# One K load cut into six: seven eighths of the row in one load, the last eighth in a load of 112 rows and four loads of 4 rows

## The chip, the cores and the metric

One core of a Trainium2 chip runs the kernel. The metric is the device time in microseconds (us) of one execution, as the median of several runs. Lower is better.

## The reference

For two batch entries with one token each, a gate mixes an attention block over a long cache (32 heads, 16384 cached positions, head size 128) with a small two-layer MLP.

```python
def _A_ref(x, k_cache, v_cache, wq, wo):
    q = (x @ wq).reshape(B, Sq, H, Dh).transpose(0, 2, 1, 3)
    scores = jnp.einsum("bhqd,bhkd->bhqk", q, k_cache) * (Dh ** -0.5)
    p = _softmax(scores, axis=-1)
    o = jnp.einsum("bhqk,bhkd->bhqd", p, v_cache)
    return o.transpose(0, 2, 1, 3).reshape(B, Sq, H * Dh) @ wo

def _B_ref(x, w1, w2, w3, w4):
    h = _gelu(_layernorm(x) @ w1)
...
    x1 = x + hs
    return x1 + _gelu(_layernorm(x1) @ w3) @ w4

g = _sigmoid((x * gate_w).sum(-1, keepdims=True))
return g * _A_ref(...) + (1 - g) * _B_ref(...)
```

All inputs are bf16. The K cache and the V cache hold 2 x 32 x 16384 x 128 numbers each, 268 MB each, and every one of them is read once.

## The kernel before

The attention is cut into 32 **units**. A unit is one batch entry `s` (0 or 1) of one pair of heads `i` (0 to 15), and its K and its V are 8 MB each. One load brings such a block to the 128 partitions: 64 KB lie in a row of DRAM for each partition, so the load has 128 rows of 64 KB. Units 0 and 1 (pair 0) are written out by hand, together with the MLP; the loop of L895 runs over the other 15 pairs, two units each; a hand-written tail holds the last V.

For a unit, VectorE transposes K in eight chunks (`dve_scores`, L640): a chunk is one eighth of each row (32 of its 256 positions, 8 KB). TensorE multiplies each transposed chunk with the query (`pe_scores`, L663), eight matmuls a chunk. There are two buffers `kt`, so that transpose number n waits for the scores of chunk n - 2. Unit 1 takes its chunks in the order of the row, so the last eighth is its last chunk. The scores are then transposed back (L647), reduced to a maximum, and turned into weights (`exponent`, L685); the product with V is L713, the projection with `wo` L758.

**The order of the loads.** All large loads are issued by SyncE (SP), on one DMA queue, and each waits on SP until its destination is free. Up to the loop they are: `wq`, `w1`, `w2`, K of unit 0 (L249), `w3`, K of unit 1 (L839), `w4` (issued in `ln.dma`, called at L844). K of unit 1 waits for the fourth transpose of unit 0 (`tr3`, L837) and for the last readers of `w1` and `w2`, whose place it takes; `w4` waits for the matmuls with `w3` (`linear`, L843; its matmuls are L531). In the loop each unit's turn is: K (L906), after the fourth transpose of the unit just before it (`tr3`; the first K of the loop thus waits for unit 1's fourth transpose), then the V of the pair before (L908), after the matmuls with the V that was there, then, once a pair, `wo` (L911, 32 rows of 16 KB to every fourth partition). ACT issues three tiny loads at the start, for the two rows of x and for the gate's row (`xrow`, issued in L82): each has 4 rows of 512 bytes, to partitions that lie 32 apart.

**What waits for K of unit 1.** The first transpose of unit 1 (L640, called at L860) waits for the semaphore `kl1` to reach 16. Behind it on VectorE stand the other transposes of unit 1, the reciprocal of `invert(u0)` (L708) and an addition (L865). The load that SP issues next but one, K of pair 1, batch 0 (L906), waits for unit 1's fourth transpose. The matmuls with `w4` (L870) stand on TensorE behind the scores of unit 1's first seven chunks.

**The tail.** The last V comes in four pieces of 128, 64, 48 and 16 positions of the row (L938), then `wo` for the last two heads in three loads (L946 to L948). The first two pieces go through L713, and VectorE's L781 and L787 reduce what they gave; the last two pieces go through L996. Then come the last projection (L758), the copies to the output row and its store.

Of the kernel before, what the change touches and what calls it, by code (L numbers as in the profile page):

```python
# [88 lines left out]
def kernel(  # L89
# [16 lines left out]
    P = nc.NUM_PARTITIONS  # L106
    B, Sq, D = A_x.shape
    _, H, Sk, Dh = A_k_cache.shape
# [8 lines left out]
    NJ = 2 * Sk // P  # L117
    CT = 32
    NCK = NJ // CT
    GT = 16  # L120
    NG = NJ // GT
    Q4 = 4
# [19 lines left out]
    def S(name):  # L142
        if name not in sems:
            sems[name] = (tc if name in ("fin", "st") else nc).alloc_semaphore(name)
        return sems[name]
# [59 lines left out]
    def region(cell, elements):  # L205
        return mem[:, cell * CELL : cell * CELL + elements]
# [4 lines left out]
    k_rows = A_k_cache.rearrange("b (g t) s d -> b g (t s d)", t=2)  # L211
# [3 lines left out]
    def unit_rows(rows, hp, s):  # L215
        if isinstance(hp, int):
            flat = rows[s, hp : hp + 1, :]
        else:
            flat = rows[s, bass.ds(hp, 1), :]
        return flat.rearrange("o (p x) -> (o p) x", p=P)  # L220
# [7 lines left out]
    def wait(engine, name, value):  # L228
        if isinstance(value, int) and value == 0:
            return  # L230
        engine.wait_ge(S(name), value)
# [7 lines left out]
    with tc.tile_critical(sync_engine=mybir.EngineType.Activation, no_gpsimd_drain=True):  # L239
        PE, DVE, ACT, POOL, SP = nc.tensor, nc.vector, nc.scalar, nc.gpsimd, nc.sync  # L240
# [10 lines left out]
        for b, row in enumerate((A_x[0, 0], A_x[1, 0], gate_w)):  # L251
# [9 lines left out]
                out=ident_f[:], in_=ident_f[:], compare_op=ALU.not_equal, fill=1.0, base=0,  # L261
# [10 lines left out]
        for k in range(2):  # L272
# [14 lines left out]
                out=lmat[:].rearrange("p (g h k) -> p g h k", h=2, k=4),  # L287
                in_=hm2[:].unsqueeze(1).unsqueeze(3).to_broadcast([P, P // 8, 2, 4]),
# [3 lines left out]
        for h in range(2):  # L292
# [4 lines left out]
                    out=place[:, at : at + P].rearrange("p (g k) -> p g k", k=2 * QP)[:, :, 0 : HB + 1 : HB],  # L297
                    in_=ident_f[:, h * HALF : (h + 1) * HALF].rearrange("p (g k) -> p g k", k=QP)[:, :, 0:B],
# [6 lines left out]
                out=ident_s[:], in0=ident_f[:], scalar1=-scale, scalar2=None, op0=ALU.mult  # L305
# [6 lines left out]
                out=rep1[:], in_=ident_f[:].rearrange("p (c k) -> p k c", k=QP), axis=AX.X, op=ALU.add  # L312
# [6 lines left out]
                out=mask4[:], in_=ident_f[:].rearrange("p (c k) -> p c k", k=QP), axis=AX.X, op=ALU.add  # L319
# [3 lines left out]
        for g in range(Q4):  # L323
# [3 lines left out]
                    out=rep4[:, g, :].rearrange("p (a k) -> p a k", k=QP),  # L327
# [13 lines left out]
                out=hsel[:], in_=rep1[:, 0:8].rearrange("p (h k) -> p h k", k=4), axis=AX.X, op=ALU.add  # L341
# [179 lines left out]
        def linear(actT, w, R, N, act_key, w_key, banks, out_keys):  # L521
# [7 lines left out]
            def one(n):  # L529
# [19 lines left out]
                out=tsc[:],  # L549
                in_=oacc2[:].rearrange("p a (m k e) -> p (a m) e k", k=QP, e=2),  # L550
# [6 lines left out]
                out=qTb[:], in_=tsc[:].rearrange("p (c k) -> p c k", k=QP)[:, :, 0:B]  # L557
# [15 lines left out]
        for e in range(2):  # L573
            rows = slice(e * HALF, (e + 1) * HALF)
# [3 lines left out]
                    out=qd[rows],  # L578
                    in_=R_ps[rows].rearrange("p (hp e v b) -> p e hp b v", e=2, v=4, b=B)[:, e],
# [24 lines left out]
        def chunk_ids(s):  # L604
            low, high = list(range(NCK // 2)), list(range(NCK // 2, NCK))
            return high + low if K_CELL[s] == 0 else low + high

        def k_view(s):
            return region(K_CELL[s], NJ * Dh).rearrange("p (j d) -> p j d", d=Dh)
# [9 lines left out]
        def pool_unit(n):  # L619
            wait(POOL, f"sc{NCK - 1}", 0 if n.first else n.after(-1))  # L620
            i, s = n.i, n.s
            dst = qw[s][:, :, NG - 1 : NG - 1 + QP * (Q4 - 1) + 1 : QP]
            row = qd[:, i, s, :] if isinstance(i, int) else qd[:, bass.ds(i, 1), s, :].rearrange("p o v -> p (o v)")
            POOL.tensor_tensor(  # L624
                out=dst,
                in0=row.unsqueeze(2).to_broadcast([P, 4, Q4]),
                in1=mask4[:].unsqueeze(1).to_broadcast([P, 4, Q4]),
                op=ALU.mult,
            ).then_inc(S("qwd"), 1)

        def dve_scores(u, first=0, last=NCK):
            s = u.s
            for n, c in list(enumerate(chunk_ids(s)))[first:last]:
                if n == 0:
                    wait(DVE, f"kl{s}", u.landed)
                if n >= 2:
                    wait(DVE, f"sc{n - 2}", u.after(1))
                else:
                    wait(DVE, f"sc{n + 6}", u.after(0))
                DVE.transpose(  # L640
                    out=kt[n % 2][:],
                    in_=k_view(s)[:, c * CT : (c + 1) * CT, :].rearrange("p j d -> p (j d)").bitcast(FP32),
                ).then_inc(S(f"tr{n}"), 1)
            if last < NCK:
                return
            wait(DVE, f"sc{NCK - 1}", u.after(1))
            DVE.transpose(out=st[:].rearrange("p j r -> p (j r)"), in_=sps[s][:]).then_inc(S("stT"), 1)  # L647
            wait(DVE, "stT", u.after(1))
            DVE.tensor_reduce(out=m_t[:], in_=st[:, :, 0:NG], axis=AX.XY, op=ALU.max).then_inc(S("mx"), 1)  # L649

        def pe_scores(u, first=0, last=NCK):
            s = u.s
            if first == 0:
                wait(PE, "qwd", u.after(1))
                wait(PE, "stT", 0 if u.first else u.after(-1))
            for n, c in list(enumerate(chunk_ids(s)))[first:last]:
                wait(PE, f"tr{n}", u.after(1))
                ktb = kt[n % 2][:].bitcast(BF16).rearrange("p (j w k e) -> p j w k e", j=CT, w=2, k=QP, e=2)
                for half in range(CT // GT):
                    m = c * (CT // GT) + half  # L660
                    for v in range(4):
                        w, e = divmod(v, 2)
                        ins = PE.matmul(  # L663
                            sps[s][:].rearrange("p (j k) -> p j k", k=QP),
                            lhsT=qw[s][:, v, NG - 1 - m : NG - 1 - m + P],
                            rhs=ktb[:, half * GT : (half + 1) * GT, w, :, e],
                            start=(n == 0 and half == 0 and v == 0),
                            stop=(n == NCK - 1 and half == CT // GT - 1 and v == 3),
                        )
                ins.then_inc(S(f"sc{n}"), 1)  # L670
# [158 lines left out]
        for key in ("qd", "mask4", "qw0", "qw1"):  # L829
# [6 lines left out]
        pe_scores(u0, 0, NCK // 2 - 1)  # L836
        wait(SP, "tr3", 1)  # L837
        ln.wait("SP", ln.needs([], ["w1", "w2"]))
        SP.dma_start(out=region(1, NJ * Dh), in_=unit_rows(k_rows, 0, 1)).then_inc(S("kl1"), 16)  # L839
        layernorm_T(x1T[:], xn2T[:], "ln2", "x1T", "xn2T")  # L840
        dve_scores(u0, NCK // 2)
        pe_scores(u0, NCK // 2 - 1, NCK - 1)
# [7 lines left out]
                out=tsc[:, 0:FQ],  # L850
                in_=oacc2[:, :, 0:half].rearrange("p a (i c) -> p c a i", c=FC),
# [5 lines left out]
        exponent(u0)  # L857
        ln.op("POOL", lambda: POOL.memset(tsc[:], 0.0), writes=["tsc"])
        pool_unit(u1)
        dve_scores(u1, 0, NCK // 2)  # L860
        pe_scores(u1, 0, NCK // 2 - 1)
        total(u0)
# [23 lines left out]
                out=brow[:], in0=brow[:], scalar1=omgrow[:, 0:1], scalar2=None, op0=ALU.mult  # L886
# [50 lines left out]
        for n, size in enumerate(PIECES):  # L937
            SP.dma_start(  # L938
                out=region(V_CELL, NJ * Dh)[:, at * Dh : (at + size) * Dh],
                in_=unit_rows(v_rows, HP - 1, 1)[:, at * Dh : (at + size) * Dh],  # L940
# [24 lines left out]
                out=rinv2[:], in0=rinv2[:], scalar1=g_rep[:, 1:2], scalar2=None, op0=ALU.mult  # L965
# [39 lines left out]
        for h in range(2):  # L1005
# [12 lines left out]
            out=out.rearrange("b s (h g c) -> g (b s) h c", h=2, g=Q4), in_=out_row[0 : P - HB + 1 : HB, :]  # L1018
# [37 lines left out]
```

## Time and profile before

| | |
|---|---|
| three runs, median (lowest to highest) | 1331.53 us (1331.51 to 1331.89) |
| the profiled execution's own time | 1331.57 us |
| its span, from its first to its last instruction | 1329.7 us |
| read from DRAM | 572.53 MB, 431 GB/s over the span |
| VectorE busy | 710.1 us (53%) |
| TensorE busy, and its mean granted clock | 824.7 us (62%), 0.801 |
| three stretches from the table by windows: 0 to 20, 130 to 1290, 1290 to 1326 us | DMA share 1.00, 1.00, 0.95 |

The DMA share is the mean busy share of the core's 16 DMA engines. A load of 128 rows puts 8 rows on each engine.

The trace also holds each packet of the DMA queues: its queue, its start, its duration and its size. The views only sum them up, but the list can be read directly. In it a load's row is one packet, and each engine closes its share of a load with a packet of 4 bytes, so that a load of 128 rows leaves 16 of these. On an engine a packet starts about 4 ns before the recorded end of the one before it, so the packets of one engine can be strung together. The list's clock runs 10.52 us ahead of that of the views (the last 4-byte packet of unit 1's K at 99.99 us there, the transpose that waits for it at 89.47 us here). What it shows, in ns:

| load | its 16 closing packets, from the earliest |
|---|---|
| `w2` (third load) | 0 18 25 44 75 88 100 102 114 134 135 195 264 279 299 354 |
| K of unit 0 | 0 17 25 43 75 97 100 102 114 150 263 279 299 354 1145 1656 |
| K of unit 1 | 0 32 33 35 73 91 102 120 183 273 289 310 344 1173 1596 1687 |
| last V, second piece | 0 83 166 263 265 321 336 417 1156 1624 1634 1650 1683 1697 1850 1934 |

| packet | median duration, ns | number |
|---|---|---|
| 65536 bytes | 2422 | 8192 |
| 57344 bytes (rows of `w3` and `w4`) | 2118 | 256 |
| 16384 bytes (among them all of `wo` in the loop) | 611, highest 624 | 864 |
| 12288 bytes | 461 | 128 |
| 4096 bytes | 159 | 128 |
| 4 bytes, closing | 9 | 1440 |
| instructions' queue, 16384 bytes | 1009 to 1221 | 8 |

From the earliest closing packet of `w3` to that of unit 1's K are 19348 ns, and to those of `w3` and `w4` from the load before each 16909 and 16938 ns; from that of the second piece of the last V to that of the third (12288 bytes a row) 3687 ns.

The 12 packets of the three tiny loads lie on four of the engines, the same four for all three loads; in the row of `w2` these four are the engines at 0, 25, 195 and 299.

### The profile page before, as it was taken

How to read it: one execution, taken by the hardware profiler on the slowest of the kernel's cores; microseconds unless marked ns; L12 is line 12 of the kernel's file. 1: busy time of each engine (PE TensorE's matmuls, PEld its weight loads, DVE VectorE, ACT ScalarE, POOL GpSimd, SP SyncE). 2: the span in 40 equal slices, each digit the busy share in tenths (PEclk: the TensorE clock that was granted, in tenths of full speed). 3: DMA queues.
4: the chain of work that ended last, by engine and by line, in shares of the span. 5: the costliest groups of instructions: out<-in, count | busy, mean ns of one | idle time of the engine just before them, and what ended most of it. 6: DMA issues, size and time to landing. Idle time of an engine off the chain costs nothing.

```text
span 1329.7 us, 14080 instructions
## 1 busy us (share of the span) xinstructions
PE 824.7 (62%) x6060; PEld 379.8 (29%) x6060; DVE 710.1 (53%) x712; ACT 105.2 (8%) x165; POOL 15.9 (1%) x47
## 2 busy tenths in 40 slices
PE   2356576665666656567665657656566766656765
PEld 0123232232332223233232323223232322323323
DVE  2365466554556654456565445665444665545561
ACT  0010000000000000000000000000000000000000
POOL 0100000000000000000000000000000000000000
PEclk9587888777888777788877778877778887778885
DMA  9999999999999999999999999999999999999998
GB/s 410 439 422 434 445 424 438 430 430 438 430 438 430 438 430 440 428 440 428 440 426 442 424 444 424 444 424 438 430 430 438 430 438 430 440 428 440 428 440 346
DMA packets 11573, 572.68 MB, mean 431 GB/s; under 512 B 1472, under 2 KB 1740, under 8 KB 1996
## 3 DMA queue, kind: packets, MB, share of 16 engines
q1 hardware_dynamic: 11520, 572.53, 99.6%
q8 instruction: 8, 0.13, 0.0%
q10 hardware_dynamic: 44, 0.01, 0.0%
q14 instruction: 1, 0.01, 0.0%
HBM read 572.53 MB, written 0.00 MB: 431 GB/s over the span
## 4 chain that ended last, share of the span: by engine, by line
DMA 68%; DVE 16%; PE 11%; issue 3%; another core or an unknown queue 1%; POOL 0%; SPq 0%; ACT 0%; POOLq 0%; ACTq 0%
DMA mem<-in_A_k_cache_dram 66%; DVE kt L640 16%; PE S L663 10%; DMA mem<-in_A_v_cache_dram 2%; PE oacc L713 0%; PE ot L531 0%; SPq L906 0%; PE R L996 0%; POOL qw L267 0%; POOL pt L269 0%; DVE st L647 0%; DVE part L787 0%; POOL ln_rstd L471 0%; PE arow L758 0%
## 5 line engine op out<-in xcount | busy, mean ns | idle before, releaser
L663 PE MATMUL S<-kt,qw 128*128 128x512 bf16 x2048 | 544.6, 415 | 265.3 <-DVE kt L640 265.0
L640 DVE STREAM_TRANSPOSE kt<-mem 128x2048 f32<-128x2048 f32 x256 | 570.3, 2282 | 168.8 <-DMA mem<-in_A_k_cache_dram 118.6
L663 PEld LDWEIGHTS S<-kt,qw 128*128 128x128 bf16 x2048 | 194.7, 104 | 601.6 <-issue 292.4
L713 PE MATMUL oacc<-mem,pt 128*8 128x512 bf16 x2032 | 120.2, 390 | 4.3 <-DMA mem<-in_A_v_cache_dram 4.3
L685 ACT ACTIVATE pt<-st,nb 64x256 bf16<-64x256 f32 x64 | 90.1, 1408 | 283.9 <-DVE nb L699 283.4
L731 PE MATMUL ot<-hsel,red 128*128 128x2 f32 x480 | 76.1, 289 | 54.7 <-DVE red L787 54.7
L731 PEld LDWEIGHTS ot<-hsel,red 128*128 128x128 f32 x480 | 73.6, 238 | 69.8 <-DVE red L787 69.8
L781 DVE TENSOR_SCALAR part<-oacc,maskr 128x128 f32<-128x128 f32 x31 | 10.9, 351 | 140.7 <-PE oacc L713 140.7
L674 ACT ACTIVATE Dm<-ident_s,m 128x128 f32<-128x128 f32 x32 | 12.8, 401 | 875.5 <-DVE m L649 875.5
L704 PE MATMUL R<-rs,lmat 128*128 128x1 f32 x64 | 18.4, 357 | 79.1 <-ACT pt L685 79.1
L713 PEld LDWEIGHTS oacc<-mem,pt 128*8 128x8 bf16 x2032 | 47.2, 88 | 64.5 <-issue 5.4
L708 DVE RECIPROCAL rinv<-R 128x1 f32<-128x1 f32 x32 | 5.4, 168 | 109.5 <-PE R L704 109.5
L647 DVE STREAM_TRANSPOSE st<-S 128x512 f32<-128x512 f32 x32 | 22.9, 717 | 70.0 <-PE S L663 70.0
L676 PE MATMUL R<-Dm,ones_f 128*128 128x128 f32 x64 | 15.6, 326 | 54.4 <-ACT Dm L674 54.4
L814 DVE TENSOR_SCALAR oa<-ot,hm 128x8 f32<-128x8 f32 x30 | 6.8, 226 | 78.9 <-PE ot L731 78.9
L704 PEld LDWEIGHTS R<-rs,lmat 128*128 128x128 f32 x64 | 15.8, 306 | 84.9 <-ACT pt L685 84.7
L758 PE MATMUL arow<-wo,OT 128*17 128x128 bf16 x960 | 28.3, 310 | 10.5 <-DVE OT L819 10.5
L685 ACT ACTIVATION_READ_ACCUMULATOR pt<-st,nb 64x1 f32 x64 | 30.7, 479 | 0.0
L676 PEld LDWEIGHTS R<-Dm,ones_f 128*128 128x128 f32 x64 | 9.5, 188 | 70.2 <-ACT Dm L674 70.2
L758 PEld LDWEIGHTS arow<-wo,OT 128*17 128x17 bf16 x960 | 24.6, 132 | 11.3 <-issue 11.3
L787 DVE SCALAR_TENSOR_TENSOR part<-oacc,maskr,part 128x128 f32<-128x128 f32 x62 | 21.8, 351 | 2.2
L624 POOL TENSOR_TENSOR qw<-qd,mask 128x16 bf16<-128x16 f32 (+1 forms) x32 | 8.3, 264 | 1117.7 <-PE S L663 1117.7
(114 smaller groups left out, 128.6 us busy)
## 6 DMA issues: line engine op xcount, KB each, us to landing
mem<-in_B_w_dram SPq DMA_DIRECT2D x2, 7168.0 KB, 34.6
wo<-in_A_wo_dram SPq DMA_DIRECT2D x15, 512.0 KB, 25.2
mem<-in_B_w_dram SPq DMA_DIRECT2D x2, 2048.0 KB, 28.4
mem<-in_A_v_cache_dram SPq DMA_DIRECT2D x1, 4096.0 KB, 21.3
mem<-in_A_v_cache_dram SPq DMA_DIRECT2D x1, 2048.0 KB, 25.8
mem<-in_A_v_cache_dram SPq DMA_DIRECT2D x1, 1536.0 KB
mem<-in_A_k_cache_dram SPq DMA_DIRECT2D x32, 28.2
mem<-in_A_v_cache_dram SPq DMA_DIRECT2D x1, 512.0 KB
```

The lines of the kernel that those rows point to most:

```text
L640: DVE.transpose(out=kt[n % 2][:], in_=k_view(s)[:, c * CT : (c + 1) * CT, :].rearrange("p j d -> p (j d)").bitcast(FP32),).then_inc(S(f"tr ...
L647: DVE.transpose(out=st[:].rearrange("p j r -> p (j r)"), in_=sps[s][:]).then_inc(S("stT"), 1)
L663: ins = PE.matmul(sps[s][:].rearrange("p (j k) -> p j k", k=QP), lhsT=qw[s][:, v, NG - 1 - m : NG - 1 - m + P], rhs=ktb[:, half * GT : (ha ...
L674: ACT.activation(out=Dm[:], in_=ident_s[:], func=ACTF.Copy, scale=m_t[:, 0:1]).then_inc(S("dm"), 1)
L676: PE.matmul(R_ps[:, 0:P], lhsT=ones_f[:], rhs=Dm[:], start=True, stop=True).then_inc(S("rr"), 1)
L685: ins = ACT.activation(out=pts[s][rows, :, e, :].rearrange("p (m a) k -> p a k m", a=GT // 4), in_=st[rows, :, 0:NG].rearrange("p (a k) m ...
L704: PE.matmul(tot_ps[:, 0:1], lhsT=lmat[:], rhs=rs_t[:], start=True, stop=True).then_inc(S("tt"), 1)
L713: ins = PE.matmul(oacc[s][QP * q : QP * q + 8, :], lhsT=pts[s][:, g].rearrange("p h k -> p (h k)"), rhs=V[:, 4 * g : 4 * g + 4, :].rearran ...
L731: ins = PE.matmul(ot_ps[:, 2 * r : 2 * r + 2], lhsT=red_t[:, r : r + 2 * P - 1 : 2], rhs=hsel[:], start=True, stop=True, skip_group_check= ...
L758: ins = PE.matmul(arow[h][QP * g : QP * g + HB + 1, :], lhsT=o[:, e, :], rhs=w[:, e, at : at + Dh], start=False, stop=stop, skip_group_che ...
L781: ins = DVE.tensor_scalar(out=part[:], in0=in0, scalar1=mask[:, 0:1], scalar2=None, op0=ALU.mult)
L787: ins = DVE.scalar_tensor_tensor(out=red[:] if twice else part[:], in0=in0.unsqueeze(1).to_broadcast([P, 2, Dh]) if twice else in0, scalar ...
```

## The change

The load of unit 1's K at L839 takes the first seven eighths of the 128 rows only (57344 bytes a row). Five loads for the last eighth (8192 bytes a row) follow on the same queue: one of the rows 0 to 111, then four of 4 rows each, the rows 112, 116, 120, 124, then 113, 117, 121, 125, and so on. The five share a new semaphore, `l_kx`. VectorE waits for all of them (80) ahead of unit 1's first transpose.

```diff
         ln.wait("SP", ln.needs([], ["w1", "w2"]))
-        SP.dma_start(out=region(1, NJ * Dh), in_=unit_rows(k_rows, 0, 1)).then_inc(S("kl1"), 16)
+        FEW, MAIN = 4, (NCK - 1) * CT * Dh
+        SP.dma_start(out=region(1, MAIN), in_=unit_rows(k_rows, 0, 1)[:, 0:MAIN]).then_inc(S("kl1"), 16)
+        most = P - Q4 * FEW
+        for rows in [slice(0, most)] + [slice(most + k, P, FEW) for k in range(FEW)]:
+            SP.dma_start(
+                out=region(1, NJ * Dh)[rows, MAIN : NJ * Dh],
+                in_=unit_rows(k_rows, 0, 1)[rows, MAIN : NJ * Dh],
+            ).then_inc(S("l_kx"), 16)
         layernorm_T(x1T[:], xn2T[:], "ln2", "x1T", "xn2T")
...
         pool_unit(u1)
+        wait(DVE, "l_kx", 16 * (1 + FEW))
         dve_scores(u1, 0, NCK // 2)
```

## The prediction

> **What bounds the kernel now.** I read the page first: the slices, the queues, the chain.
>
> ```profile
> span 1329.7 us, 14080 instructions
> ...
> DMA  9999999999999999999999999999999999999998
> ...
> q1 hardware_dynamic: 11520, 572.53, 99.6%
> q8 instruction: 8, 0.13, 0.0%
> ...
> HBM read 572.53 MB, written 0.00 MB: 431 GB/s over the span
> ...
> DMA 68%; DVE 16%; PE 11%; issue 3%; another core or an unknown queue 1%; POOL 0%; SPq 0%; ACT 0%; POOLq 0%; ACTq 0%
> ```
>
> The 16 DMA engines are busy from the first slice to the last, and 99.6% of that is SP's one queue. So the span is the bytes of the engine that finishes last, plus the work after its last landing. The chain, read in order of time, shows where that is decided at the end, and what stands around the edit:
>
> ```profile
> 64.15 25.30 DMA mem<-in_A_k_cache_dram
> 89.44 0.02 issue
> 89.47 2.32 DVE kt L640
> ...
> 100.00 25.91 DMA mem<-in_A_k_cache_dram
> 125.90 0.02 issue
> ...
> 1294.10 25.82 DMA mem<-in_A_v_cache_dram
> 1319.92 0.04 issue
> 1319.97 1.91 PE oacc L713 x12
> ```
>
> Unit 1's K is issued at 64.15 and its transposes begin at 89.47; the end hangs on the second piece of the last V, which lands at 1319.92. A landing is the slowest of 16 engines. The third view is the timeline of SP's queue:
>
> ```profile
> 28.37 0.33 SPq L82 DMA_DIRECT2D mem<-in_B_w_dram  x1
> 64.15 0.33 SPq L839 DMA_DIRECT2D mem<-in_A_k_cache_dram  x1
> 78.85 0.33 SPq L82 DMA_DIRECT2D mem<-in_B_w_dram  x1
> 100.00 0.35 SPq L906 DMA_DIRECT2D mem<-in_A_k_cache_dram  x1
> 112.38 0.34 SPq L908 DMA_DIRECT2D mem<-in_A_v_cache_dram  x1
> ```
>
> Each load is issued well before the one ahead of it is through: `w4`'s last closing packet is at 106.41 us, 6.4 us after L906's issue. The queue never runs dry, so an engine that falls behind stays behind to the end. The list of packets shows this: of the closing packets of the last V's second piece eight lie within 0.42 us, one is at 1.16 and seven at 1.62 to 1.93 us. A step of about 1.5 us comes from one instruction-queue packet (1009 ns or more) plus a longer packet behind it (2886 to 2968 ns for 2422). The engine at 1.16 got its lateness before the edit, at 37.2 us of the span, from an 8 KB instruction packet of 309 ns and a longer packet after it (3039 ns).
>
> **The change, part by part.** *Bytes per engine.* A load of 4 rows puts one row on each of four engines, and the three tiny loads put theirs on the same four each time; so I take these four for all four small loads. 112 rows are 7 on each of 16 engines. Instead of 8 rows' last eighth the four engines carry 7 + 4 = 11 and the other twelve 7. A row of 8192 bytes is not in this queue before; by its neighbours, 4096 bytes at 159 - 4 = 155 ns and 12288 at (3687 - 5) / 8 = 460 ns, it takes the middle, 308 ns. A closing packet costs 9 - 4 = 5 ns. Per engine:
>
> - removed: one load of 8 x 64 KB, 19348 ns (from `w3`'s first closing packet to this load's);
> - added to all: 8 x 56 KB, 16909 (`w3`) to 16938 (`w4`), say 16924, then 7 x 308 + 5 = 2161, together 19085: **-263 ns** on twelve engines;
> - added to the four: 4 x (308 + 5) = 1252 more: 20337, **+989 ns**.
>
> The four are the engines that were at 0, 25, 195 and 299 ns in `w2`'s row. Followed packet by packet to the end, three are among the eight early ones (at most 321) and the fourth is the one at 1156: its instruction packet fell on the engine at 195. So at the end the latest of the twelve comes to 1934 - 263 = 1671, three of the four to 321 + 989 = 1310 at most, and the fourth to 1156 + 989 = 2145. The last landing moves by 2145 - 1934 = **+0.21 us**. It is paid in full, as everything behind 1319.92 hangs on it and the later pieces move with the same engine.
>
> [...]
>
> *Five more issues on SP.* One takes 0.33 (L839) to 0.54 us (L249), so 1.7 to 2.7 us, done by 64.15 + 6 x 0.54 = 67.4 us. Cost 0: SP next stands until 78.85 for TensorE's `w3` matmuls. Without those 11 us it would delay `w4`, whose place in the queue falls due only when unit 1's K ends.
>
> *The wait on VectorE.* `kl1` alone would now be met 2 us sooner, but `l_kx` stands behind it. Unit 1's K was complete at 1687 ns of its row, with the fourth engine at 1173; now it is complete at 1173 + 989 = 2162, so the first transpose starts 0.48 us later, near 89.95. Behind it on VectorE wait unit 1's transposes, L708 and L865, on TensorE the scores and `w4`'s matmuls, and on SP L906, from 100.00 to 100.48. Cost 0: the queue holds work until 106.4. The cover left is 5.9 us; every us past it would be an idle us of 16 engines. L908 (112.38) has until 125.90. The wait itself: 0.02 us ("issue").
>
> Sum: 1331.57 + 0.21 = 1331.78 for an execution like the profiled one, which is 0.04 above the median of the runs; so **1331.74 us**, no change. What a measurement of this kernel can tell from no change is about 0.2%, 2.7 us.
>
> **The rivals.**
>
> *A gain by balance.* The engine at 1156 owes this to one early instruction packet. If that falls on none of the four in the changed kernel, the latest is one of the twelve: -0.26 us, 1331.27. For it: the change alters the instruction streams. Against: the packet comes before the edited load is issued. More cannot be had: the sixteen lags average 0.94 us, so even a perfect levelling gives 1.0 us, and faster by 2.7 is shut out.
>
> *An instruction packet on one of the four, later.* Six of the eight come after the edit, each so far on an engine of its own. On one of the three early: 1310 + 1550 - 1934 = +0.9; on the fourth: 2145 + 1550 - 1934 = +1.8; so 1332.4 to 1333.3. Against: the same loop fetches the same code.
>
> *Slower: two engines writing into one place.* In a load of 128 rows each engine has partitions of its own. In the new loads the shares are cut otherwise, and the four write to partitions 112 to 127 while the engines that own these go on with `w4`. If two writers share one rate, each 8 KB packet takes 308 ns more: 11 x 308 = 3.39 us on the four, 0.21 + 3.39 = +3.6, 1335.1 us. It leaves "no change" when a packet costs (2660 - 210) / 11 = 223 ns more, 0.53 us instead of 0.31. If it hits the four small loads alone: 4 x 308, 1333.0 us. Against: `wo` in the loop puts two rows of 16 KB on each engine, to every fourth partition, also a cut unlike the others, and none of the 864 packets of that size took over 624 ns (median 611).
>
> [...]
>
> *The small loads' rows all on one engine.* That engine then has 7 + 16 rows: 16924 + 2161 + 4 x (4 x 308 + 5) - 19348 = +4.7 us. From the lag 0 that ends 2.7 us later than now, from 1156 3.9: 1334.3 to 1335.4. Against: the tiny loads.
>
> *A fixed price for each small load.* If the engines stood still while each is set up: four issues take 1.76 us at the last V (L938), so 0.44 each, 5 x 0.44 = 2.2: 1333.9. Against: there, seven loads queued in 3.2 us, and the packets follow each other with no gap. [...]
>
> **How the numbers follow.** Forecast 0.48, balance 0.2, later instruction packet 0.08, two writers 0.11 (0.07 for the full price), one engine 0.03, fixed price 0.04, anything else 0.06, half of it slower. Slower by over 0.2%: 0.07 + 0.03 + 0.03 + 0.03 = 0.16; faster 0.02; within 0.82. The range goes from below the balance case, 1331.1, to the later instruction packet on the fourth engine, 1333.3, which takes in the small loads' collision; outside lie the two slow rivals and part of the fixed price.
>
> **What would show it.** 112 packets of 8192 bytes and 16 more, each near 310 ns, with the 16 on four engines; in the closing packets of `l_kx`' last load four engines about 1.25 us later against the others than before; L640's first transpose of unit 1 near 89.95; DMA slices still 9; the landing ahead of L713's last matmuls 0.2 us later. A packet above 0.5 us, a gap in the queue near 90 to 110 us, or more than 11 rows on an engine would make it wrong.

## The result, and the profile after

The changed kernel takes 1336.38 us (1335.49 to 1337.79, 7 runs) against 1331.53 (1331.25 to 1331.89, 7 runs): 4.85 us more, a ratio of 1.0037, 95% interval 1.0027 to 1.0047. The profiled execution is the longest of the seven, 1337.79 us.

The page of the changed kernel, its span, slices and queues:

```profile
span 1335.9 us, 14085 instructions
...
DMA  9999999999999999999999999999999999999997
GB/s 408 437 379 428 433 432 434 434 434 434 434 432 434 434 434 436 432 434 432 434 433 435 436 432 432 436 432 431 439 430 436 432 434 436 432 434 434 432 436 327
...
q1 hardware_dynamic: 11680, 572.53, 99.5%
...
HBM read 572.53 MB, written 0.00 MB: 429 GB/s over the span
```

The bytes are the same and the engines are busy as before, all along. But in one slice, the third (67 to 100 us), they move 379 GB/s. The engines were not idle there, they were slow. The table by windows puts the two kernels side by side (each engine's busy time, then the granted clock, the DMA share and GB/s). Before:

```profile
66.00:86.00 20.00, 12.82 (x106) 5.01 (x104) 13.36 (x17) 1.13 (x3) 2.06 (x4) 0.97 0.99 428
86.00:106.00 20.00, 12.13 (x48) 4.85 (x49) 15.17 (x9) 2.33 (x4) 0.00 (x0) 0.78 0.99 429
```

After:

```profile
66.00:86.00 20.00, 12.45 (x104) 4.87 (x102) 13.29 (x16) 1.50 (x3) 1.84 (x4) 0.92 0.97 408
86.00:106.00 20.00, 8.40 (x26) 3.27 (x26) 8.99 (x4) 1.95 (x4) 0.00 (x0) 0.57 1.04 374
```

In the second window the DMA share is 1.04 and the rate 374 instead of 429 GB/s: over 20 us some 1.1 MB are missing, 2.5 us of the queue; the first window lacks 0.4 MB, some 0.9 us. (A packet counts in these windows where it starts, so the shares are rough.) SP's queue and VectorE around the edit, from the timeline after:

```profile
63.78 0.33 SPq L840 DMA_DIRECT2D mem<-in_A_k_cache_dram  x1
64.16 3.13 SPq L843 DMA_DIRECT2D mem<-in_A_k_cache_dram  x5
78.48 0.35 SPq L82 DMA_DIRECT2D mem<-in_B_w_dram  x1
106.32 0.36 SPq L914 DMA_DIRECT2D mem<-in_A_k_cache_dram  x1
```

```profile
84.89 0.23 DVE L699 TENSOR_REDUCE nb<-R 64x1 f32<-64x64 f32 x1
94.78 4.50 DVE L640 STREAM_TRANSPOSE kt<-mem 128x2048 f32<-128x2048 f32 x2 [9.67 <-DMA mem<-in_A_k_cache_dram]
```

The six issues are through at 67.3 us. Unit 1's first transpose starts at 94.78 instead of 89.47, so the K of the loop's first unit is issued at 106.32 instead of 100.00. The queue still holds work then: `w4` is through at 108.7 us on the first engine and at 112.1 on the last. Yet the issue comes late for some engines. By the list of packets, four of them wait for their first row of that K, 2.6 us together, and nine first rows take 2646 to 3545 ns instead of 2422. From `w4`'s closing packets to those of this K the mean engine needs 20.00 us, before 19.45. The end still hangs on the last V, now on its last two pieces instead of the second (the chain after):

```profile
1301.46 28.63 DMA mem<-in_A_v_cache_dram
1330.09 0.05 issue
1330.14 1.88 PE R L1004 x64
```

The list of packets shows the loss at its place. (In it the transpose's 94.78 us is 104.69.) Durations in ns:

| packets | before | after |
|---|---|---|
| 128 of 8192 bytes, last eighth of unit 1's K: lowest, median, highest | | 309, 528, 854 |
| the longest of 57344 bytes in `w4` | 2127 | 4501, 4487, 4413, 4372 ... |
| packets of 57344 bytes over 2300, in K and `w4` | 0 | 27 |
| mean over the 16 engines, from `w3`'s closing packets to `w4`'s | 36377 | 40355 |

The 8 KB packets took 30.5 us more together than at 309 ns each, the 56 KB packets of K and `w4` 32.8 us more than at 2121: 63.3 us over 16 engines, 3.96 us each, nearly all of the 3.98 us of the last row. It falls between the start of the first 8 KB packet and the end of the last one, 8.9 us. In that time the engines together went at little more than half their rate, also those that carried nothing but their 7 rows and were already at `w4`: the ten rows of `w4` that began in the middle of it took 4102 to 4501 ns instead of 2120.

### The profile page after: what moved, and what is told of

Its sections match the earlier page's. It is cut to its first block, busy times and chain, and to the rows that moved or that the text cites. A ratio compares the mean times of both kernels' runs of the same rounds, so it can differ in the third digit from the quotient of the medians.

```text
span 1335.9 us, 14085 instructions
## 1 busy us (share of the span) xinstructions
PE 826.0 (62%) x6060; PEld 377.5 (28%) x6060; DVE 711.2 (53%) x712; ACT 105.4 (8%) x165; POOL 15.9 (1%) x47
## 4 chain that ended last, share of the span: by engine, by line
DMA 68%; DVE 14%; PE 13%; issue 3%; another core or an unknown queue 1%; SPq 0%; POOL 0%; ACT 0%; POOLq 0%; ACTq 0%
DMA mem<-in_A_k_cache_dram 66%; DVE kt L640 14%; PE S L663 12%; DMA mem<-in_A_v_cache_dram 2%; PE ot L531 0%; PE oacc L713 0%; SPq L843 0%; SPq L914 0%; PE R L1004 0%; POOL qw L267 0%; POOL pt L269 0%; SPq L946 0%; DVE st L647 0%; POOL ln_rstd L471 0%
## 5 line engine op out<-in xcount | busy, mean ns | idle before, releaser
L663 PE MATMUL S<-kt,qw 128*128 128x512 bf16 x2048 | 551.8, 420 | 268.6 <-DVE kt L640 268.3
L663 PEld LDWEIGHTS S<-kt,qw 128*128 128x128 bf16 x2048 | 197.5, 105 | 609.3 <-issue 308.7
L731 PE MATMUL ot<-hsel,red 128*128 128x2 f32 x480 | 70.7, 278 | 54.7 <-DVE red L787 54.7
L731 PEld LDWEIGHTS ot<-hsel,red 128*128 128x128 f32 x480 | 68.1, 222 | 69.8 <-DVE red L787 69.8
```

Source lines behind the costliest of these rows:

```text
L663: ins = PE.matmul(sps[s][:].rearrange("p (j k) -> p j k", k=QP), lhsT=qw[s][:, v, NG - 1 - m : NG - 1 - m + P], rhs=ktb[:, half * GT : (ha ...
L731: ins = PE.matmul(ot_ps[:, 2 * r : 2 * r + 2], lhsT=red_t[:, r : r + 2 * P - 1 : 2], rhs=hsel[:], start=True, stop=True, skip_group_check= ...
```

## The experiments

Each was timed against the kernel before on the same chip. Of each edit only the line that chooses the rows is shown; VectorE's wait counts the loads. The kernels without "extra" in their name differ from the changed kernel in this line. All kernels that carry "extra" leave K of unit 1 as it was and add loads of the last eighth of some of its rows to an 8 KB stretch of each partition that is free at that time; VectorE waits for them at the same place. "Mean" is the last row of the table above, less 36.38 us. A "row of `w4`" is a packet of 57344 bytes.

| kernel | time, us | ratio, 95% interval | 8 KB packets, ns: lowest, median, highest | longest row of `w4`, ns | mean, us |
|---|---|---|---|---|---|
| changed | 1336.38 | 1.0027 to 1.0047 | 309, 528, 854 | 4501 | +3.98 |
| split_only | 1331.61 | 0.9991 to 1.001 | 309, 313, 322 | 2587 (one) | +0.09 |
| rows112_16 | 1335.08 | 1.0018 to 1.0038 | 309, 546, 835 | 4131 | +3.38 |
| few_first | 1335.13 | 1.0017 to 1.0038 | 309, 588, 914 | 3951 | +3.58 |
| halves64 | 1335.87 | 1.0021 to 1.0046 | 309, 626, 962 | 4249 | +4.37 |
| few_adjacent | 1336.84 | 1.0023 to 1.0052 | 309, 572, 989 | 4900 | +4.46 |
| extra_few_high | 1334.36 | 1.0012 to 1.0032 | 309, 617, 646 | 3912 | +1.72 |
| extra_few_64 | 1334.08 | 1.0011 to 1.003 | 309, 623, 647 | 3569 | +1.81 |
| extra_few_low | 1332.42 | 0.9997 to 1.0016 | 309, 310, 316 | 2127 | +0.32 |
| extra_few_32 | 1332.16 | 0.9995 to 1.0014 | 309, 311, 316 | 2129 | +0.32 |
| extra_two_high | 1332.77 | 0.9999 to 1.0019 | 309, 533, 649 | 3346 | +1.27 |
| extra_64_by_2 | 1332.68 | 0.9999 to 1.0019 | 309, 309, 321 | 2138 | +1.26 |
| extra_112 | 1336.65 | 1.0024 to 1.0053 | 309, 525, 866 | 4120 | +5.35 |

The kernel before had medians of 1331.51 to 1331.59 us beside them.

**1. split_only: the cut along the row alone.**

```diff
-        for rows in [slice(0, most)] + [slice(most + k, P, FEW) for k in range(FEW)]:
+        for rows in [slice(0, P)]:
```

> Unit 1's K in two loads of 128 rows: seven eighths and the last eighth. Theory A (two engines that write into the same group of partitions slow each other, and every engine behind them): rows stay with their engines, so packets of 8192 bytes take about 310 ns and the time is that of before within 0.3 us. Theory B (short pieces of rows that lie far apart in DRAM are slow to read, wherever they go): the 128 packets take about 530 ns as in the changed kernel, +1.8 us or more. Theory C (each load on few engines has a price): as before within 0.3 us.

The time is that of before and the 128 packets take 313 ns. VectorE's timeline in this kernel:

```profile
89.78 4.50 DVE L640 STREAM_TRANSPOSE kt<-mem 128x2048 f32<-128x2048 f32 x2 [4.69 <-DMA mem<-in_A_k_cache_dram]
```

So neither short packets, nor one more load, nor the wait for `l_kx` costs anything here; theory B is out.

**2. rows112_16: no engine carries more than another.**

```diff
+        for rows in [slice(0, 112), slice(112, P)]:
```

> The last eighth in a load of 112 rows and one of 16 rows, one row on each engine, so no engine carries more than another. Theory A: the 112 rows, 7 to an engine, cross from one group of partitions into the next; packets of 8192 bytes between 310 and 700 ns, the 16 engines lose 1.5 to 3 us, time +1.5 to +3 us. Theory B: as in the changed kernel's first part, about +2 us, and the same in the load cut only by columns. Theory C: as before within 0.3 us.

+3.6 us, somewhat over the 1.5 to 3 that theory A had said, though here no engine carries more rows than another: most of the price isn't the uneven load, and theory C, a price of loads on few engines, doesn't explain it.

**3. and 4. extra_few_high and extra_few_low: one source, two places.**

```diff
+        for rows, source in [(slice(112 + k, P, 4), slice(112 + k, P, 4)) for k in range(4)]:
```

```diff
+        for rows, source in [(slice(k, 16, 4), slice(112 + k, P, 4)) for k in range(4)]:
```

> The K load as before in one piece; behind it four extra loads of 4 rows of 8192 bytes, from the same source rows 112 to 127, to partitions 112 to 127 of a stretch that nobody reads. Theory A: the four engines write to partitions that four others own; the extra packets take about 600 ns and the first rows of w4 on all engines about 4300 ns instead of 2120, so +2 to +3 us. Theory B: the same. Theory C: the same or less.

> The same four extra loads from the same source rows, but to partitions 0, 4, 8, 12, then 1, 5, 9, 13, and so on. Theory A: if the four engines are those that own these partitions in a load of 128 rows, nobody meets anybody: packets about 310 ns, w4's rows 2120 ns, time within 0.5 us of before. Theories B and C: the same loss as with partitions 112 to 127.

VectorE's timelines, first high, then low:

```profile
92.39 2.31 DVE L640 STREAM_TRANSPOSE kt<-mem 128x2048 f32<-128x2048 f32 x1 [6.49 <-DMA mem<-in_A_k_cache_dram]
```

```profile
90.22 4.51 DVE L640 STREAM_TRANSPOSE kt<-mem 128x2048 f32<-128x2048 f32 x2 [4.70 <-DMA mem<-in_A_k_cache_dram]
```

The same bytes from the same DRAM rows, by the same four engines, in loads of the same shape; only the partitions differ. To 0 to 15 every packet takes 309 to 316 ns and no row of `w4` over 2127. To 112 to 127 they take up to 646, and ten rows of `w4` take 3309 to 3912 (about 4300 had been expected). This decides for theory A against B and C: it counts where the rows go. The low kernel's mean, +0.32 us, is its bytes (16 x 310 / 16 = 0.31). That its time rose by 0.91, more than the 0.5 expected, fits the uneven load: four engines carry 1.25 us more, and `w4`'s closing packets spread over 2.57 us instead of 1.69. The mean engine also lost 0.13 us behind `w4`; the next K was issued only 3.0 us before `w4` was through on the first engine.

**5. few_first: the change with its few rows on free places.**

```diff
+        for rows in [slice(16, P)] + [slice(k, 16, 4) for k in range(4)]:
```

> As the changed kernel, but the four small loads bring rows 0 to 15 (0, 4, 8, 12, then 1, 5, 9, 13 and so on) and the load of 112 rows the rows 16 to 127. Theory A: the small loads are free of meetings, so that only the 112 rows pay. The 112 rows' packets as in the changed kernel, 310 to 700 ns; once they are through, the small loads' packets take about 310 ns and w4's rows 2120 ns. Time between before and the changed kernel, +1.5 to +3.5 us. If the price were the number of loads or of engines: +4.8 us, as the changed kernel.

+3.6 us. The 112 rows alone pay most of the price. The small loads' packets took about 550 ns all the same, and the rows of `w4` 3476 to 3951: two late engines were still at their 112-load rows until the last small load was nearly through. So packets were held up (about 550 ns) that went to the partitions where extra_few_low took 309 to 316 ns; theory A had expected these to be free.

**6. halves64: two times 64 rows, 4 to an engine.**

```diff
+        for rows in [slice(0, 64), slice(64, P)]:
```

> The last eighth in two loads of 64 rows, 0 to 63 and 64 to 127, 4 rows to an engine in each, so all engines carry as much as before. Theory A with shares handed out as consecutive rows: the partitions of 64 rows belong to eight engines, sixteen write there, so that each packet takes about 620 ns in place of 310; 8 x 310 = 2.5 us lost on all, +2.5 us, more if w4's rows are held up too. Theory A with shares handed out by place: 310 ns and the time of before within 0.3 us.

The packets take 626 ns at the median, twice 310, as the first reading had said, but the loss is 4.4 us, not 2.5: `w4`'s first rows are held up too, 3604 to 3878 ns on thirteen engines and 4249 at most in K itself, until three late engines are through. If the places of all engines lie like those of the four in 3., 4., 8. and 9. (0 to 15 and 32 to 47 free, 64 to 79 and 112 to 127 not), 64 adjacent rows lie on half of the places, so this run alone doesn't tell how shares are handed out.

**7. few_adjacent: the four rows of a small load side by side.**

```diff
+        for rows in [slice(0, 112)] + [slice(112 + 4 * k, 116 + 4 * k) for k in range(4)]:
```

> As the changed kernel, but each small load brings four rows that lie next to each other (112 to 115, then 116 to 119, 120 to 123, 124 to 127). Theory A: the four engines write into one group of four partitions at once, beside its owner; the small loads' packets take 4 x 310 = 1240 ns or more, the four engines lose about 4 x 0.6 us more than in the changed kernel, time +6 to +9 us against before. If the place of the rows does not matter: as the changed kernel, +4.8 us.

A miss: 1336.84 us is within half a us of the changed kernel, and the longest packet took 989 ns, not 1240. Four adjacent rows on the four engines cost little more than four rows that lie 4 apart, which a plain sharing of one place's rate would not give.

**8. and 9. extra_few_32 and extra_few_64: which places are free.**

```diff
+        for rows, source in [(slice(32 + k, 48, 4), slice(112 + k, P, 4)) for k in range(4)]:
```

```diff
+        for rows, source in [(slice(64 + k, 80, 4), slice(112 + k, P, 4)) for k in range(4)]:
```

> The four extra loads of 4 rows behind an unchanged K load, to partitions 32, 36, 40, 44, then 33, 37, 41, 45, and so on. Theory A with the places of an engine lying 32 apart in a load of 128 rows (four rows, and the four that lie 32 further): these belong to the same four engines as 0 to 15, packets about 310 ns, time as with partitions 0 to 15, +0.9 us. Theory A with eight consecutive rows to an engine: 32 to 47 belong to others, packets about 600 ns, +2 to +3 us as with 112 to 127.

> The four extra loads of 4 rows behind an unchanged K load, to partitions 64 to 79. If the four engines' own places are 0 to 15 and 32 to 47 only: as with 112 to 127, packets up to 600 ns and more, +2 to +3 us. If 112 to 127 were a special place (the last 16 partitions) and any other were free: packets about 310 ns, +0.6 to +0.9 us as with 0 to 15.

Partitions 32 to 47 were as free for the four engines as 0 to 15 (8 KB packets of 311 and 310 ns at the median), 64 to 79 as dear as 112 to 127 (623 and 617 ns).

**10. extra_two_high: two engines only.**

```diff
+        for rows, source in [(slice(112 + k, 117 + k, 4), slice(112 + k, 117 + k, 4)) for k in range(4)]:
```

> An unchanged K load, then four extra loads of 2 rows only, to partitions 112 and 116, then 113 and 117, 114 and 118, 115 and 119: two engines write beside two owners. If a meeting slows only those who meet: extra packets about 600 ns, and first rows of w4 of 3000 ns and more on two to four engines, about 2120 ns on the other twelve; the time within 1.5 us of before. If a meeting holds up every engine, as the traces so far look: w4's first rows long on twelve or more engines, mean loss over the engines 1 to 1.5 us, time +1.5 to +2.5 us.

The list of packets, rows of `w4` longer than 2135 ns, start and duration in ns:

```
 98596 3201    98687 3196    98713 3200    98721 3201    98746 3196
 98781 3201    98810 3346    98836 3198    98840 3198    99003 3196
 99099 3198    99937 2982   100782 2539   101047 2432   101633 2268
```

The eight extra packets ran from 98781 to 101045. Of the eleven rows that began in or just ahead of that time, ten are longer by the same 1.08 us (3198 - 2120) and one by 1.23, whichever engine they are on: about half of 2.26 us. Two 64 KB rows of K that were still under way are longer by as much (3494 and 3505 for 2422). The extra packets themselves start at the usual price and get longer: 309 and 320 ns for the first of each engine, 392 and 439 for the second, 627 to 649 for the others. Two engines with four packets each took 1.1 us from all sixteen (mean +1.27, less 8 x 310 / 16 = 0.16 of bytes). The time, +1.25 us, is below the 1.5 to 2.5 expected for this and would fit "slows only those who meet" as well, but the long rows are those of "holds up every engine".

**11. and 12. extra_64_by_2 and extra_112: which shapes are clean.**

```diff
+        for rows, source in [(slice(0, P, 2), slice(0, P, 2))]:
```

```diff
+        for rows, source in [(slice(0, 112), slice(0, 112))]:
```

> An unchanged K load and one extra load of 64 rows, every second one (0, 2, 4, ... 126), to those partitions: 4 rows to an engine, 4 x 310 = 1.24 us of bytes on each. If shares are handed out so that rows spread evenly over all partitions keep their places (as the packets of wo, 32 rows on every fourth partition, suggest): packets about 310 ns, w4's rows 2120 ns, time +1.2 to +1.4 us. If shares are consecutive rows, an engine's four rows cover two places and engines meet: packets about 600 ns, +2.5 to +5 us.

> An unchanged K load and one extra load of rows 0 to 111, 7 to an engine: 7 x 310 = 2.2 us of bytes on each. With meetings as in the changed kernel: packets of 310 to 800 ns, the first rows of w4 long until the last packet is through; loss beyond the bytes 2.5 to 3.5 us, time +4.5 to +5.7 us. If the 112 rows alone were harmless and only the 16 rest rows did the damage: +2.2 to +2.5 us.

The windows, first of extra_64_by_2, then of extra_112:

```profile
86.00:106.00 20.00, 11.62 (x42) 4.44 (x42) 13.69 (x8) 2.00 (x4) 0.00 (x0) 0.71 1.03 442
```

```profile
86.00:106.00 20.00, 7.52 (x26) 2.97 (x26) 8.89 (x4) 2.49 (x4) 0.00 (x0) 0.60 1.02 368
```

Every second row, 64 of them, was clean: 309 ns, a mean of 4 x 310 = 1.24 us, nothing else. 112 rows cost 5.35 us of mean, 2.17 of it bytes, so 3.2 us of meetings. Read by places, what counts is the shape of the load, not its length: the shares of 64 rows spread evenly kept their places (309 ns at the median), those of 64 adjacent rows didn't (626 in halves64), nor did those of 112 (525). The list of packets holds no partitions, so this is inferred from the durations.

No variant was faster than before. Every load tried here whose rows go to other engines' places cost time; the queue has no time at which the owner of a place rests (DMA share 0.99 from 66 to 106 us in the kernel before).

## Why the prediction was wrong, point by point

**The bound: right.** The time is DMA throughput, the engines stay busy (9 in all slices but the last), and the tail hangs on the last V, which lands at 1330.09 us.

**Issues on SP: right. The wait: its cost of 0 failed.** The issues were done at 67.3 us (said: 67.4). The wait moved the first transpose by 5.3 us, not 0.48, as the loads themselves were late; in split_only, where they were not, issue, wait and cut cost nothing. The prediction let the queue hold work until `w4`'s last closing packet and asked for no lead. In the changed kernel the next K was issued 5.8 us before that, but only 2.4 us before `w4` was through on the first engine, and the mean engine lost 0.55 us there (20.00 less 19.45). In all kernels with a lead of 3.3 us or more over the first engine the stretch took 19.44 to 19.45 us; with 2.4 to 3.1 us (the changed kernel, few_adjacent, extra_few_low, extra_few_32) it took 0.09 to 0.55 more. The lead as the cause is argued from this order; no run moved the issue alone.

**Rows to the engines: right.** Eleven 8 KB rows on four engines, seven on twelve; the load of 112 rows left 16 closing packets, the four small ones 4 each.

**The price of an 8 KB row: this step failed.** "308 ns" held for a row that meets nobody (309 to 322 in split_only, extra_few_low, extra_64_by_2). In the changed kernel the median was 528, and the step had no term at all for the rows of `w4` and of K that ran beside them, more than half of the loss. The sum said +0.05 us for the mean engine (4 x 0.989 less 12 x 0.263, over 16); it was +3.98.

**"Two engines writing into one place": the nearest rival, at 0.11.** It named the right condition, rows that go to another engine's partitions, and its 1335.1 us is 1.3 short. That it came so near is in part luck, as two things in it were wrong. It charged only those who write, 11 packets on four engines, when a meeting took a third to a half of the rate of all sixteen for as long as it lasted (1.1 us of 2.3 in extra_two_high, 1.4 of 3.9 in extra_few_high, 4.0 of 8.9 in the changed kernel). And it was put down for a row of `wo`: "a cut unlike the others, and none of the 864 packets took over 624 ns". That showed only that nothing was lost there, not that engines had met there without loss. extra_64_by_2 shows why it can't be used: by its durations (309 to 321 ns), rows spread evenly over the partitions kept their places, so by this reading `wo` has no meetings to show.

**The uneven load, +0.21 us: too small.** extra_few_low has the uneven load and no meetings. There, at the closing packets of the last V's first piece, the latest engine is 1.48 us behind the mean one, before 0.99: 0.49 us more. For the changed kernel it can't be separated. The mean loss of 3.98 us is that of the profiled execution, which took 6.22 us more than the profiled one before (1337.79 against 1331.57). With the 0.55 us above, 1.7 us are left; the latest engine's lag at the same place is 2.93 us, 1.94 more than before. In it come together the uneven load, what single engines lost in meetings, and later instruction packets, the rival at 0.08. How the 4.85 us of the median divide is open, as only the longest execution was profiled.

**The other rivals.** A fixed price for each small load is out: one load more cost 0.1 us in split_only, and in extra_64_by_2 the time rose by 1.09 us, less than its 1.24 of bytes. The 0.03 that this rival has among the chances of slower by over 0.2% needs some 0.49 us a load ((2.66 - 0.21) / 5), which no run shows; the price worked out for it, 0.44, falls short of that. All small rows on one engine: no, they lie on four. A gain by balance did not show.

**What stays open.** Why a meeting slowed engines that weren't part of it. Also, whether it takes an owner that writes at the same time, or whether writing away from one's own partitions is enough: in every run the owners were writing, and the miss of few_adjacent speaks against a plain sharing of one place. Also open is how 112 rows are handed out.

## What to carry to other kernels

On this queue, which keeps all engines busy, a load was not only bytes per engine. It also counted where its rows went: 8 KB from the same four engines took 310 ns at the median to partitions 0 to 15 and 617 to 112 to 127, and where packets met, by this reading, in extra_two_high, extra_few_high and the changed kernel, all sixteen lost a third to a half of their rate while it lasted. Where a load is to be cut, try first 128 rows, or rows spread evenly over the 128: here they took 313 and 309 ns a row and cutting along the row was free, while cutting the rows into 112 + 16 cost 3.6 us for 1 MB. And before a quiet row of the trace is taken as proof that a collision is harmless, make sure that there was a collision in it.

## What the runs showed of the hardware that was not expected

- Beside two engines writing four 8 KB rows each to partitions 112 to 119 (extra_two_high), ten of eleven rows of `w4` took 1.08 us longer, and the eleventh 1.23.
- In the changed kernel a load issued on a queue that still held work for 2.4 us on its first engine came late for some engines: four waited, 2.6 us together, and nine first rows took 2646 to 3545 ns for 2422.
- For the four engines that serve loads of 4 rows, partitions 0 to 15 and 32 to 47 were free (309 to 316 ns for 8 KB), 64 to 79 and 112 to 127 were not (medians of 623 and 617, up to 647).
- In the kernel before, an instruction packet of 1009 to 1099 ns cost its DMA engine about 1.5 us, as the data packet behind it was longer too (2886 to 2968 ns for 2422). These lags stayed to the end, and a late engine also prolonged a meeting for the others: in halves64 three late engines were still writing 8 KB rows about 2.5 us after the others had begun `w4`, whose first rows took 3604 to 3878 ns on thirteen engines.
